# Causal attention with chosen experts on one core: the order of the diagonal key blocks inside a run of value sums

## The chip, the core and the metric

The kernel runs on one core of one Trainium2 chip. The metric is the device time of one execution in microseconds (us), as the median of several runs. The profile is of one more execution of the same kernel; its span runs from the first instruction to the last.

## What is computed

Two stages follow each other. The first is a linear attention: queries and keys are sketched with S1 and S2, multiplied out to 64 features, and summed against the values. Its output x (batch 4, 1088 tokens, 128 columns) goes into the second stage, a causal softmax attention with four experts of which each token takes two:

```python
for e in range(E):                       # 4 experts, heads of 64
    q, k, v = x @ wq[e], x @ wk[e], x @ wv[e]
    scores = scale * (q @ k.transpose(0, 2, 1))
    scores = np.where(causal, -1e9, scores)
    a = softmax(scores)
    ye = a @ v @ wo[e]
    out += (the share of e, where e is one of a token's two) * ye
```

The kernel uses that q k^T = x (wq wk^T) x^T and that a v wo = (a x)(wv wo): the weights are multiplied once, and what remains per batch is scores of x against x and sums of x weighted by a. The change touches these sums.

## The kernel before, in words

**Tiling.** A batch has 17 tiles of 64 tokens. For each tile the two chosen experts make two rows per token, so a score tile has 128 rows. The 17 tiles form three groups (`groups`, line 141): tiles 0 to 5, 6 to 11 and 12 to 16. A group has one buffer AT with its softmax weights, turned so that keys lie on partitions; one run of value sums per group and batch multiplies AT with x.

**A run of value sums** is `values` (line 1111). It goes over key steps j of 32 keys, J = 2·t1 of them: 12, 24 and 34 for the three groups. The 128 rows of AT are four bands of 32 rows, g = 0 to 3, one for each chosen expert and half of a tile's tokens; each j issues one matmul per band (line 1129), with 32 rows of x as weights and up to 32·nt columns of AT moving, nt being the tiles of the group (6, 6, 5). A full matmul is thus 192, 192 or 160 columns wide. The four bands use four different rows of the TensorE array and four different PSUM banks. All matmuls are float32, and the profile shows each as two passes, each with its own weight load.

**Causality.** `first(j, h)` (line 1119) gives the first column that key step j can reach: tiles ahead of it are skipped. Up to j = 2·t0 a matmul is full; from there on, in the diagonal part, it loses 32 columns with every second j, down to 32 columns. For odd j the bands with h = g % 2 = 0 (g = 0 and 2) lose 32 columns more, and at j = J−1 they have nothing to do, so that j issues two matmuls alone.

**Blocks and jobs.** A run is cut into blocks of four j (lines 1135 to 1140), each a job of the planner. A job reads the block before it, AT, and the x rows of its keys: tiles xr0 (j 0 to 11), xr1 (j 12 to 23) and xr2 (from j 24), named xra, xrb and xrc in the profile. The last block makes ("V", b, n), on which the copies out of PSUM wait: `keep`, `patch`, `mix` (lines 1148 to 1161).

**Order.** `ORDER` (line 21) is a fixed list of job numbers in the order in which the jobs are issued; a job's number is the place at which it was created. Each engine takes its instructions in that order. TensorE's work beside the sums is, above all, the scores (line 1053), the queries of the experts (line 1015), the output products (lines 1200, 1226, 1250) and the first stage of the next batch (lines 528, 577, 714, 769, 821). They use other shapes of the array than the sums' 32 rows by 128 columns: most of them 128 by 128.

**Runs in the order of time.** Batches 0 to 2 sum their groups as 0, 1, 2; batch 3 as 1, 2, 0. Mostly a run stands alone between other work. In batch 1, group 2 follows group 1 with nothing between, and other TensorE work stands behind group 2's fourth and sixth blocks. In batch 3, other work stands behind group 1's third block; what is left of group 1, group 2 and group 0 then follow one another with nothing between.

Of the kernel before, what the change touches and what calls it, by code (L numbers as in the profile page):

```python
# [71 lines left out]
class Plan:  # L72
# [5 lines left out]
    def job(self, name, eng, us, f, reads=(), makes=None, holds=(), landing=0.0, mode="", rank=0.0):  # L78
        eng = (eng,) if isinstance(eng, str) else tuple(eng)
        us = (us,) * len(eng) if isinstance(us, float) else tuple(us)  # L80
        self.jobs.append(dict(name=name, eng=eng, us=us, f=f, reads=tuple(reads), makes=makes, holds=tuple(holds),
                              landing=landing, mode=mode, rank=rank, n=len(self.jobs)))
# [32 lines left out]
def kernel(  # L115
# [76 lines left out]
    def copy(eng, o, i):  # L192
        (nc.scalar.copy if eng == "ACT" else VEC[eng].tensor_copy)(o, i)  # L193

    def d_us(n):
        return 0.18 + n / 960

    def a_us(n):
        return 0.2 + 0.00073 * n

    def p_us(n):
        return 0.12 + 0.0022 * n
# [799 lines left out]
    def masks_of(b, n, *xs):  # L1002
        return [("mb", b, n, x) for x in xs] if b == 0 and n == 0 else [("mb", b, n, 0)]
# [107 lines left out]
    def values(b, n, rank):  # L1111
        t0, t1 = groups[n]
        nt = t1 - t0
        w = 64 * nt
        AT, agg, mb = ("AT", b, n), ("agg", b, n), ("mb", b, n)
        Vk = [("ps", "V", b, n, l) for l in range(2)]
        J = 2 * t1

        def first(j, h):

            return 32 * max(0, j // 2 - t0) + (32 if j % 2 and j // 2 >= t0 and h == 0 else 0)

        def block(j0, j1):
            a = plan[AT][:, 0 : J * nt * 32].rearrange("p (j t s) -> p j (t s)", t=nt, s=32)
            for j in range(j0, j1):
                for g in range(4):
                    rows, lo = slice(32 * g, 32 * g + 32), first(j, g % 2)
                    if lo < 32 * nt:
                        nc.tensor.matmul(plan[Vk[g // 2]][:, g % 2, lo : 32 * nt], plan[(f"xr{j // 12}", b)][rows, j % 12], a[rows, j, lo:],  # L1129
                                         start=(j == 0), stop=(j == J - 2 + g % 2))  # L1130

        def cost(j0, j1):
            return sum(max(2 * (32 * nt - first(j, 1)) / 1200, 0.105 if j == J - 1 else 0.21) + 0.005 for j in range(j0, j1))

        for j0 in range(0, J, 4):
            j1 = min(j0 + 4, J)
            need = [("AT", b, n), ("xr", b, j0 // 12)] + ([("V", b, n, j0)] if j0 else [])
            job(f"sum {b}.{n}.{j0}", "PE", cost(j0, j1), lambda e, j0=j0, j1=j1: block(j0, j1), need,
                ("V", b, n, j1) if j1 < J else ("V", b, n),
                [AT, *Vk, (f"xr{j0 // 12}", b)], mode="V", rank=rank + 0.001 * j0)  # L1140

        def by_half(a):
            return a[:, 0:w].rearrange("p (t h s) -> p h t s", h=2, s=32)

        def sums_of(l):
            return plan[Vk[l]][:, :, 0 : 32 * nt].rearrange("p h (t s) -> p h t s", s=32)

        def keep(e, x):
            copy(e, by_half(plan[agg][:, x]), sums_of(x % 2))

        def patch(x):
            nc.vector.copy_predicated(by_half(plan[agg][:, 2 + x]), by_half(plan[mb][:, 4 + x].bitcast(U16)), sums_of(1 - x))

        def spread_sums(x):
            a = plan[agg][:, 2 * x : 2 * x + 2, 0:w]
            nc.gpsimd.tensor_tensor(out=a, in0=a, in1=plan[mb][:, 2 * x : 2 * x + 2, 0:w], op=ALU.mult)  # L1156

        r = rank + 0.1
        if last_group(b, n):
            def mix(x):  # L1160
                nc.vector.tensor_tensor(out=by_half(plan[agg][:, x]), in0=sums_of(x), in1=by_half(plan[mb][:, x]), op=ALU.mult)

            def scale_one(e, x):
                a = plan[agg][:, 2 + x, 0:w]
                VEC[e].tensor_tensor(out=a, in0=a, in1=plan[mb][:, 2 + x, 0:w], op=ALU.mult)

            for x in range(2):
                job(f"keep V {b}.{n}.{2 + x}", ("ACT", "DVE"), (a_us(w), d_us(w)), lambda e, x=x: keep(e, 2 + x),
                    [("V", b, n)], ("aggk", b, n, 2 + x), [Vk[x], agg], rank=r)
                job(f"mix V {b}.{n}.{x}", "DVE", d_us(w), lambda _, x=x: mix(x), [("V", b, n), *masks_of(b, n, 0)], ("agg", b, n, x),  # L1170
                    [Vk[x], agg, mb], rank=r + 0.01 * x)
                job(f"patch V {b}.{n}.{x}", "DVE", d_us(w), lambda _, x=x: patch(x),
                    [("V", b, n), ("aggk", b, n, 2 + x), *masks_of(b, n, 2)], ("aggp", b, n, x), [Vk[1 - x], agg, mb], rank=r + 0.01)
                job(f"scale V {b}.{n}.{x}", ("POOL", "DVE"), (p_us(w), d_us(w)), lambda e, x=x: scale_one(e, x),
                    [("aggp", b, n, x), *masks_of(b, n, 1)], ("agg", b, n, 2 + x), [agg, mb], rank=r + 0.02)
            return
        for x in (2, 3, 0, 1):
            job(f"keep V {b}.{n}.{x}", ("ACT", "DVE"), (a_us(w), d_us(w)), lambda e, x=x: keep(e, x),
                [("V", b, n)], ("aggk", b, n, x), [Vk[x % 2], agg], rank=r)
        for x in range(2):  # L1180
            job(f"patch V {b}.{n}.{x}", "DVE", d_us(w), lambda e, x=x: patch(x),
                [("V", b, n), ("aggk", b, n, 2 + x), *masks_of(b, n, 2)], ("aggp", b, n), [Vk[1 - x], agg, mb], rank=r + 0.01)
        for x in range(2):
            need = [("aggk", b, n, 0), ("aggk", b, n, 1)] if x == 0 else [("aggp", b, n)]
            job(f"spread V {b}.{n}.{x}", "POOL", p_us(2 * w), lambda e, x=x: spread_sums(x),
                [*need, *masks_of(b, n, x)], ("agg", b, n), [agg, mb], rank=r)

    def last_group(b, n):
        return b == B - 1 and n == 0
# [85 lines left out]
    def batch(b):  # L1275
        base = 100.0 * b
        order = []
        seq = list(range(NG)) if b < B - 1 else [1, 2, 0]
        for n in seq:
            order.append(("q", n))  # L1280
            for i in range(*groups[n]):
                order.append(("s", i))
        at, x = {}, 0.0
        for kind, y in order:
            at[(kind, y)] = base + x
            x += 2.6 if kind == "q" else (64 * (y + 1)) / 600 + 0.9 * (1 + y // 6)
        sc = 88.0 / x
        for kk in at:
            at[kk] = base + (at[kk] - base) * sc
        for n, (t0, t1) in enumerate(groups):  # L1290
            queries(b, n, at[("q", n)] - 14)
            for i in range(t0, t1):
                scores(b, n, i, at[("s", i)] - 3)
            p = seq.index(n)
            vt = at[("s", groups[seq[p + 1]][0] + 1)] if p + 1 < NG else base + 96
            values(b, n, vt)
            outputs(b, n, vt + 6)
# [42 lines left out]
```

## Time and profile before

| | |
|---|---|
| time, median of 3 runs | 263.02 us (262.99, 263.02, 263.62) |
| the profiled execution's own time | 263.14 us |
| its span | 261.4 us |
| granted TensorE clock | 1.000 |
| matmuls of line 1129 | 1136 with xra, 752 with xrb, 304 with xrc, two for each float32 product |

The profile names PE for TensorE's matmuls and PEld for its weight loads, DVE for VectorE, ACT for ScalarE and POOL for GpSimd. A timeline row gives start, duration, engine, line, what is written and read, the array shape, the moving operand's shape and how many instructions are merged in the row (x4); the duration of a merged row reaches from the first start to the last end. Starts are recorded, while the ends of matmuls are modelled. Where a row merges matmuls of several widths, it shows the first one's. A row of the table by stretches gives the stretch, its length, PE's busy time and count and PEld's, the granted clock and the DMA traffic.

### The profile page before, as it was taken

The page shows a single profiled execution, that of the slowest core. Times are in us where ns is not written, and L with a number is a line of the kernel's source. Part 1 is how long each engine was busy: PE and PEld are TensorE (multiplying, and loading weights), DVE is VectorE, ACT ScalarE, POOL GpSimd, SP SyncE. Part 2 cuts the span into 40 slices and gives each one's busy share as a digit, 9 for nine tenths or more (in the row PEclk, how much of TensorE's full clock was granted, in tenths as well). Part 3 has the DMA queues.
Part 4 walks back from the last instruction along what each step waited for, and adds up shares of the span by engine and source line. Part 5 has one row for each costly group of instructions (what it writes and reads, how often), then busy time and mean ns, then how long its engine had stood idle before and what let it go on. Part 6 is the DMA issues. An engine that isn't in the chain of part 4 may idle for free.

```text
span 261.4 us, 9228 instructions
## 1 busy us (share of the span) xinstructions
PE 253.7 (97%) x3811; PEld 189.7 (73%) x3813; DVE 212.8 (81%) x541; ACT 100.4 (38%) x268; POOL 155.8 (60%) x255
## 2 busy tenths in 40 slices
PE   7799999999999999999999999999999999999994
PEld 2388656666598895765799776665796885889994
DVE  4988999979989968999988379799989569881743
ACT  2183545563542406426432041825222515611220
POOL 3569479937498635498652794556435654442660
PEclk9999999999999999999999999999999999999999
DMA  6989379813736566903417592304560396240003
GB/s 207 162 180 165 80 173 151 175 39 81 172 72 109 115 148 141 190 20 118 81 39 114 143 204 54 109 0 73 103 119 0 91 217 159 44 111 6 5 0 88
DMA packets 85194, 27.84 MB, mean 106 GB/s; under 512 B 56736, under 2 KB 84128, under 8 KB 85152
## 3 DMA queue, kind: packets, MB, share of 16 engines
q1 hardware_dynamic: 84560, 26.56, 49.4%
q8 instruction: 30, 0.49, 0.8%
q10 hardware_dynamic: 592, 0.69, 0.7%
q14 instruction: 12, 0.10, 0.1%
HBM read 22.62 MB, written 4.62 MB: 104 GB/s over the span
## 4 chain that ended last, share of the span: by engine, by line
PE 78%; DVE 8%; POOL 5%; DMA 4%; issue 3%; SPq 0%; ACTq 0%; ACT 0%; DVEq 0%; POOLq 0%
PE pair L1053 26%; PE pair L1129 25%; PE pair L1015 9%; PE pair L1250 7%; DMA mb<-me 3%; PE pair L1200 2%; PE pair L577 2%; DVE qs L1028 2%; POOL fp L536 2%; PE pair L528 2%; PE pair L769 2%; DMA in<-in_q_dram 1%; PE pair L1226 1%; POOL agg L1156 1%; PE pair L821 1%
## 5 line engine op out<-in xcount | busy, mean ns | idle before, releaser
L1096 POOL TENSOR_SCALAR w<-w,rs,sh 128x448 f32<-128x448 f32 (+16 forms) x68 | 55.5, 823 | 36.9 <-DVE rs L1092 33.1
L1053 PE MATMUL pair<-xT,qs 128*128 128x384 f32 (+11 forms) x216 | 74.1, 477 | 0.8 <-DVE qs L1028 0.7
L1081 ACT ACTIVATE w<-w,mx 128x192 f32<-128x192 f32 (+15 forms) x68 | 52.5, 773 | 58.0 <-DVE mx L1065 45.0
L1053 PEld LDWEIGHTS pair<-xT,qs 128*128 128x128 f32 x216 | 38.7, 190 | 26.9 <-issue 11.5
L1065 DVE CUSTOM_DVE_ANT_0 w<-pair,mask 128x768 f32<-128x768 f32 (+15 forms) x68 | 48.4, 722 | 4.7 <-PE pair L1053 3.8
L1101 DVE STREAM_TRANSPOSE AT<-w 128x832 f32<-128x832 f32 (+15 forms) x68 | 50.8, 760 | 0.5 <-POOL w L1096 0.5
L1129 PEld LDWEIGHTS pair<-AT,xra 32*128 32x128 f32 x1136 | 42.0, 185 | 4.1 <-DVE mx L1065 2.0
L1129 PE MATMUL pair<-AT,xra 32*128 32x160 f32 (+5 forms) x1136 | 44.6, 302 | 0.0
L1156 POOL TENSOR_TENSOR agg<-agg,mb 128x768 f32<-128x768 f32 (+1 forms) x22 | 34.1, 1559 | 8.9 <-ACT agg L193 5.1
L1015 PE MATMUL pair<-xT,Mq 128*128 128x384 f32 (+1 forms) x96 | 35.0, 478 | 0.0
L536 POOL TENSOR_TENSOR fp<-w 128x576 f32<-128x576 f32 x25 | 30.6, 1235 | 3.9 <-DVE w L531 2.9
L193 ACT COPY agg<-pair 128x384 f32<-128x384 f32 (+1 forms) x28 | 11.8, 462 | 47.4 <-PE pair L1129 36.9
L1129 PE MATMUL pair<-AT,xrb 32*128 32x160 f32 (+5 forms) x752 | 27.2, 287 | 0.0
L1129 PEld LDWEIGHTS pair<-AT,xrb 32*128 32x128 f32 x752 | 26.4, 185 | 0.9 <-issue 0.9
L1028 DVE COPY_PREDICATED qs<-mb,pair 128x768 f32<-128x768 uint16 (+1 forms) x24 | 23.1, 964 | 4.1 <-DMA mb<-me 3.1
L1015 PEld LDWEIGHTS pair<-xT,Mq 128*128 128x128 f32 x96 | 17.2, 190 | 10.2 <-issue 2.8
L1250 PEld LDWEIGHTS pair<-Mo,agg 128*128 128x128 f32 x168 | 20.1, 192 | 1.7 <-POOL w L743 0.5
L1250 PE MATMUL pair<-Mo,agg 128*128 128x128 f32 x168 | 20.9, 277 | 0.0
L193 DVE COPY agg<-pair 128x384 f32<-128x384 f32 (+1 forms) x18 | 9.3, 530 | 13.7 <-PE pair L1129 11.6
L1089 POOL TENSOR_SCALAR rs<-zs 128x1 f32<-128x1 f32 x28 | 5.9, 212 | 20.1 <-ACT w L1081 13.5
L531 DVE STREAM_TRANSPOSE w<-pair 128x576 f32<-128x576 f32 x16 | 11.7, 757 | 4.4 <-PE pair L528 4.4
L1081 ACT ACTIVATION_READ_ACCUMULATOR w<-w,mx 128x1 f32 x68 | 12.9, 190 | 0.0
(172 smaller groups left out, 291.7 us busy)
## 6 DMA issues: line engine op xcount, KB each, us to landing
xra<-xd SPq DMA_DIRECT2D x16, 192.0 KB, 4.6
xrb<-xd SPq DMA_DIRECT2D x16, 192.0 KB, 4.1
xrc<-xd SPq DMA_DIRECT2D x16, 160.0 KB, 3.7
mb<-me SPq DMA_DIRECT2D x3, 576.0 KB, 5.1
mb<-me SPq DMA_DIRECT2D x6, 288.0 KB, 5.1
in<-in_k_dram SPq DMA_DIRECT2D x12, 136.0 KB, 4.7
in<-in_q_dram SPq DMA_DIRECT2D x3, 544.0 KB, 4.0
xd<-w SPq DMA_DIRECT2D x12, 136.0 KB, 2.8
```

The source lines that it names most:

```text
L193: (nc.scalar.copy if eng == "ACT" else VEC[eng].tensor_copy)(o, i)
L536: VEC[e].tensor_tensor(out=f, in0=a[:, :, None, R : 2 * R].to_broadcast([128, NJ, R, R]), in1=a[:, :, 0:R, None].to_broadcast([128, NJ, R, ...
L1015: nc.tensor.matmul(plan[ps[x]][:, y, 0:w], Mq[:, ((1, 2), (0, 3))[x][y]], plan[xT][:, 64 * t0 : 64 * t1], start=True, stop=True)
L1028: nc.vector.copy_predicated(chosen(), rows(c), rows(plan[ps[x]]))
L1053: nc.tensor.matmul(plan[p][:, y, 0 : c1 - c0], plan[qs][:, 128 * t : 128 * t + 128], plan[xT][:, c0:c1], start=True, stop=True)
L1065: nc.vector.tensor_tensor_reduce(out=o, in0=src, in1=msk, scale=-1.0, scalar=mx[:, b, i, x - 1 : x] if x else 3e38, op0=ALU.add, op1=ALU.m ...
L1081: nc.scalar.activation(out=a, in_=a, func=ACTF.Exp, bias=mx[:, b, i, last : last + 1], scale=-1.0, accum_out=zs[:, b, i : i + 1])
L1096: nc.gpsimd.tensor_scalar(out=a, in0=a, scalar1=rs[:, b, i : i + 1], scalar2=plan[("sh", b)][:, i : i + 1], op0=ALU.mult, op1=ALU.mult)
L1101: nc.vector.transpose(dst[:, 0 : keys // 32, t], plan[A][:, 0:keys].rearrange("p (j s) -> p j s", s=32))
L1129: nc.tensor.matmul(plan[Vk[g // 2]][:, g % 2, lo : 32 * nt], plan[(f"xr{j // 12}", b)][rows, j % 12], a[rows, j, lo:], start=(j == 0), sto ...
L1156: nc.gpsimd.tensor_tensor(out=a, in0=a, in1=plan[mb][:, 2 * x : 2 * x + 2, 0:w], op=ALU.mult)
L1250: nc.tensor.matmul(plan[p][0:m, 0, 128 * x : 128 * x + 128], plan[agg][:, e, 128 * x : 128 * x + m], Mo[:, e], start=(e == 0), stop=(e == ...
```

## The change

The blocks of a run are put in another order. `starts` holds the first j of each block; the first `whole` of them, max(1, t0 // 2), stay as they are, and the rest are turned round. Inside a turned block j falls instead of rising.

| group | blocks before | blocks after |
|---|---|---|
| 0 (12 j) | 0, 4, 8 | 0, 8↓, 4↓ |
| 1 (24 j) | 0, 4, 8, 12, 16, 20 | 0, 4, 8, 20↓, 16↓, 12↓ |
| 2 (34 j) | 0, 4, ... 20, 24, 28, 32 | 0, 4, ... 20, 32↓, 28↓, 24↓ |

The last matmul of a run was 32 columns wide; it is now 128 in group 0 (j = 4), 192 in group 1 (j = 12) and 160 in group 2 (j = 24). The first block, with the matmuls that start the accumulation, stays first. The set of matmuls, their operands and their number are the same, and so is `ORDER`: the job at each place of a run now issues the block that the new order has there.

```diff
+        starts = list(range(0, J, 4))
+        whole = max(1, t0 // 2)
+        starts = starts[:whole] + starts[whole:][::-1]
+
         def block(j0, j1):
             a = plan[AT][:, 0 : J * nt * 32].rearrange("p (j t s) -> p j (t s)", t=nt, s=32)
-            for j in range(j0, j1):
+            for j in range(j0, j1) if j0 in starts[:whole] else range(j1 - 1, j0 - 1, -1):
                 for g in range(4):
                     rows, lo = slice(32 * g, 32 * g + 32), first(j, g % 2)
                     if lo < 32 * nt:
                         nc.tensor.matmul(plan[Vk[g // 2]][:, g % 2, lo : 32 * nt], plan[(f"xr{j // 12}", b)][rows, j % 12], a[rows, j, lo:],
-                                         start=(j == 0), stop=(j == J - 2 + g % 2))
+                                         start=(j == 0), stop=(j == starts[-1]))
...
-        for j0 in range(0, J, 4):
+        for y, j0 in enumerate(starts):
             j1 = min(j0 + 4, J)
-            need = [("AT", b, n), ("xr", b, j0 // 12)] + ([("V", b, n, j0)] if j0 else [])
+            need = [("AT", b, n), ("xr", b, j0 // 12)] + ([("V", b, n, y)] if y else [])
             job(f"sum {b}.{n}.{j0}", "PE", cost(j0, j1), lambda e, j0=j0, j1=j1: block(j0, j1), need,
-                ("V", b, n, j1) if j1 < J else ("V", b, n),
-                [AT, *Vk, (f"xr{j0 // 12}", b)], mode="V", rank=rank + 0.001 * j0)
+                ("V", b, n, y + 1) if y + 1 < len(starts) else ("V", b, n),
+                [AT, *Vk, (f"xr{j0 // 12}", b)], mode="V", rank=rank + 0.004 * y)
```

## The prediction

> **What bounds the kernel now.** I read the first part of the page, the chain that ended last, and the list of who waited for whom on PE.
>
> ```profile
> span 261.4 us, 9228 instructions
> PE 253.7 (97%) x3811; PEld 189.7 (73%) x3813; DVE 212.8 (81%) x541; ACT 100.4 (38%) x268; POOL 155.8 (60%) x255
> ...
> PE 78%; DVE 8%; POOL 5%; DMA 4%; issue 3%; SPq 0%; ACTq 0%; ACT 0%; DVEq 0%; POOLq 0%
> PE pair L1053 26%; PE pair L1129 25%; PE pair L1015 9%; PE pair L1250 7%; DMA mb<-me 3%; PE pair L1200 2%; PE pair L577 2%; DVE qs L1028 2%; POOL fp L536 2%; PE pair L528 2%; PE pair L769 2%; DMA in<-in_q_dram 1%; PE pair L1226 1%; POOL agg L1156 1%; PE pair L821 1%
> ```
>
> ```profile
> PE pair L1053 <- DVE qs L1028: 0.7, 2, 0.5
> ```
>
> PE is busy for 97% of the span, a quarter of the chain is the sums themselves (L1129), and PE's scores wait for another engine twice, 0.7 us in all. So a gap or a saving between two PE instructions shows nearly one to one in the time. Next come the stretches of the sums, their bounds read from the timeline:
>
> ```profile
> 56.16:59.28 3.12, 3.11 (x92) 3.07 (x92) 1.00 0.22 66
> 70.88:77.90 7.02, 7.01 (x188) 6.97 (x188) 1.00 0.40 101
> 89.48:98.47 8.99, 8.98 (x268) 8.94 (x268) 1.00 0.57 117
> 108.46:111.58 3.12, 3.10 (x92) 3.07 (x92) 1.00 0.67 130
> 133.92:145.37 11.45, 11.44 (x316) 11.27 (x316) 1.00 0.45 77
> 146.90:149.29 2.39, 2.38 (x64) 2.21 (x64) 1.00 0.49 111
> 151.30:153.77 2.47, 2.45 (x76) 2.42 (x76) 1.00 1.09 181
> 167.90:171.02 3.12, 3.11 (x92) 3.07 (x92) 1.00 0.19 42
> 185.85:192.87 7.02, 7.01 (x188) 6.97 (x188) 1.00 0.61 113
> 204.02:213.01 8.99, 8.98 (x268) 8.94 (x268) 1.00 0.67 168
> 230.25:234.37 4.12, 4.11 (x96) 3.89 (x96) 1.00 0.72 173
> 235.42:250.37 14.95, 14.93 (x452) 14.90 (x452) 1.00 0.02 5
> ```
>
> Equal runs take equal time in every batch (3.12, 7.02, 8.99), at clock 1.00: they wait for nothing inside. Of the twelve stretches, nine end with a 32-column matmul today; the fifth, sixth and eleventh stop at a full one and stay as they are.
>
> **The price of one pass.** Each band of 32 rows works through its own passes. In the narrow part the loads of one pair of bands set the pace:
>
> ```profile
> 58.59 0.32 PEld L1129 LDWEIGHTS pair<-AT,xra 32*128 32x128 f32 x8
> 58.70 0.31 PEld L1129 LDWEIGHTS pair<-AT,xra 32*128 32x128 f32 x6
> 58.81 0.31 PEld L1129 LDWEIGHTS pair<-AT,xra 32*128 32x128 f32 x4
> 58.93 0.31 PEld L1129 LDWEIGHTS pair<-AT,xra 32*128 32x128 f32 x4
> ```
>
> They start every 0.112 us (0.34 us over three steps, rounded rows), whatever the width of the matmul. For a wide matmul the streaming sets it: the eleventh stretch is 24 passes of 192 columns in 4.12 us; less 0.112 for its first load and 0.09 for its end (next fence), a pass is 0.163 us, or 0.85 ns a column. So a pass costs the larger of 0.112 and 0.85 ns times its width, and the two are equal at 132 columns. Now the two kinds of end, a narrow one and two full ones:
>
> ```profile
> 59.05 0.19 PEld L1129 LDWEIGHTS pair<-AT,xra 32*128 32x128 f32 x1
> 59.28 0.13 PEld L714 LDWEIGHTS pair<-zx,S2r 128*64 128x64 f32 x1
> ```
>
> ```profile
> 234.10 0.34 PE L1129 MATMUL pair<-AT,xra 32*128 32x192 f32 x4
> 234.38 0.43 PE L1053 MATMUL pair<-xT,qs 128*128 128x192 f32 x1
> ```
>
> ```profile
> 149.05 0.31 PE L1129 MATMUL pair<-AT,xrb 32*128 32x160 f32 x4
> 149.29 0.59 PE L1015 MATMUL pair<-xT,Mq 128*128 128x384 f32 x1
> ```
>
> Narrow: the last load starts at 59.05, its matmul can stream at 59.16, 32 columns last 0.027, and the next work's load starts 0.09 later, at 59.28. At 192 columns: the last of the four matmuls starts at 234.12, streams 0.163 until 234.285, and the next work starts 0.09 later. At 160: 149.07 plus 0.136 and again 0.09. The reader is to see that the next shape's load starts some 0.09 us after the stream has ended, and never under it, however wide the last matmul is.
>
> Hence a run costs 0.112, plus the larger price for each pass but the last, plus 0.85 ns a column for the last, plus 0.09. The bands h = 1 have the most passes: group 0 has 4 of 192, 4 of 160 and 16 narrow; group 1 has 28, 4 and 16; group 2 has 52 of 160 and 16. That gives 3.10, 7.01 and 8.97 us, against 3.12, 7.02 and 8.99. The twelfth stretch (half of group 1, group 2, group 0 in one piece) comes to 14.94 against 14.95, and it holds two jumps from 32 columns back to full ones: a rise costs nothing of its own.
>
> **The change part by part.**
>
> 1. *The end.* Before, the last narrow pass has no further load of its shape behind it and costs 0.027 instead of 0.112. After, all narrow passes stand in the middle and cost 0.112, and the last wide one costs what it cost anyway. In groups 1 and 2 a run gets 0.112 − 0.027 = 0.085 longer; in group 0, which ends at 128 columns (0.109), 0.085 − 0.003 = 0.082.
> 2. *The fall* from full width to 32 columns: the load of the first narrow pass (0.112) lies under the last full matmul (0.163 or 0.136): nothing. Without that cover it would cost 0.112 a run.
> 3. *The matmuls of j = J−1*, in two bands alone: the other two bands have fewer and narrower passes, and these two passes now run beside idle bands at the start of the narrow part instead of at the end: nothing. If the idle bands had to catch up, 2 × 0.112 a run, the bound from above.
> 4. *Waits and queues.* The first block still waits for AT; the x tiles are first touched and last read in the same order, xra, xrb, xrc, so the DMAs that refill them on SP start as before, behind the same last block. Places in `ORDER`, and so every engine's queue, are the same. Nothing, up to one late landing of xrc.
> 5. *The copies out of PSUM* start with the end of the run, so 0.085 later, as PE's next work does. In the fifth stretch, where group 2 follows group 1, PE loses nothing, but group 1's sums are complete 0.085 later against PE.
>
> The nine ends: group 0 four times, group 1 twice, group 2 three times: 4 × 0.082 + 5 × 0.085 = 0.753 us on PE. Does it all arrive? The chain leaves PE at two places:
>
> ```profile
> 141.15 0.57 DVE agg L193
> ...
> 145.11 1.65 POOL agg L1156
> ...
> 147.20 6.72 DMA mb<-me
> ...
> 156.25 1.00 DVE qs L1028
> 157.25 0.04 issue
> 157.29 1.02 PE pair L1053 x2
> ```
>
> This detour starts with group 1's sums in batch 1. Four narrow ends lie ahead (0.334), and its start is 0.085 later still: 0.419. PE's own way to 157.29 has the seventh stretch on it, also 0.419. Nothing is absorbed.
>
> ```profile
> 171.16 0.48 ACT L193 COPY agg<-pair 128x384 f32<-128x384 f32 x1 [1.63 <-PE pair L1129]
> 171.19 0.54 DVE L193 COPY agg<-pair 128x384 f32<-128x384 f32 x1
> ```
>
> ```profile
> 171.02 1.34 PE L1015 MATMUL pair<-xT,Mq 128*128 128x320 f32 x4
> 172.20 2.32 PE L1200 MATMUL pair<-agg,Mo 128*128 128x320 f32 x8
> 175.03 0.67 PE L1053 MATMUL pair<-xT,qs 128*128 128x480 f32 x1 [0.52 <-DVE qs L1028]
> ```
>
> Here PE idles 0.52 us until DVE is done, so the eighth stretch's 0.082 counts only as far as DVE is late: its copy at 171.19 began when the sums were complete, to 0.03 (ACT's began at 171.16), so 0.05 to 0.082 come through. I take 0.05, a loss of 0.03. The sum: 0.753 − 0.03 = 0.72, and 263.14 + 0.72 = **263.86 us**. The profiled execution lies 0.12 above the median of 263.02 and within the three runs' spread; seen from the median, the same step ends at 263.74. The two stand on both sides of 263.81, where a change of 0.3% (about what a measurement of this kernel can tell from no change) begins.
>
> **The rivals.**
>
> *The next load hides under the wide end* (faster). Were the next work's load drawn under the last full matmul, each of the nine ends from 59.28 on would save the 0.09 and a load of 0.112 and lose 0.085: −0.117 × 9 = −1.05, 262.1 us. Against it stand both full ends above, with 0.09 left over after 192 and after 160 columns. For it: neither was followed by every kind of work that follows the nine.
> The Trainium skill ("TensorE: Matmul & The Clock Gate", "Step-by-step: what each phase is for") states that TensorE pulls weight loads ahead of matmuls in flight; by that rule this rival would hold. Its page "TensorEngine Tiling (Array Packing)", "Key Properties", says that changing the tiling mode drains the engine, and the two full ends agree with this one, 0.09 us past the stream. Chance 0.08.
>
> *The delay is absorbed.* If the detours at 141 and 171 do not move with PE, PE's 0.52 us of idling at 175 takes in all that was lost ahead of it, and 0.082 + 2 × 0.085 = 0.25 remain: 263.4 us. Against it: both detours begin with a read of what PE has just made. Chance 0.08.
>
> *The idle bands hold the others* (slower). If the idle bands of j = J−1 hold the others, two passes a run come on top, from the first turned run on: 0.72 + 9 × 0.224 = 2.7, 265.9 at most; half of it, one pass a run, is 264.9. Against it: at the end of a run the same two passes run at the same 0.112 (58.81, 58.93). Chance 0.10.
>
> *It does not do what it says:* in group 0 the run ends at 128 columns, under the 132 from which streaming sets the pace, so even a hidden load would lie there under 0.109. That is part of the forecast (0.082 instead of 0.085), not a case of its own.
>
> **How the numbers follow.** The forecast has 0.74, own range 263.5 to 264.2 (the sum from either base, 263.74 and 263.86, with 0.3 for the scatter of runs). It is split at 263.81, a little more above, since the sum's own base is the profiled time: 0.40 slower, 0.34 same. The faster rival adds 0.08 to faster, absorption 0.08 to same, the last one 0.10 to slower: faster 0.08, same 0.42, slower 0.50. The range 263.2 to 264.8 holds the forecast, absorption and the milder half of the slow case.
>
> **What would show it.** Nine stretches of sums longer by 0.08 (3.20, 7.10, 9.07), the fifth, sixth and eleventh unchanged. After each run the next shape's load 0.09 us behind the stream of a 128, 160 or 192 wide matmul; if instead it begins less than 0.2 us after the start of the last 192 wide pass, the first rival holds. Idling at 175 still near 0.5. Loads in the rising part 0.112 apart; more would be the third rival. The prediction is wrong if the runs do not get longer, or if they do and the span does not follow.

## The result, and the profile after

| | before | after |
|---|---|---|
| median | 263.19 us (16 runs, 262.87 to 263.94) | 264.11 us (16 runs, 262.98 to 265.37) |
| profiled execution: time, span | 263.14, 261.4 us | 264.11, 262.3 us |
| ratio | | 1.003, 95% interval 1.0016 to 1.0045 |

The change makes the kernel slower by 0.3%, or 0.79 us with an interval of 0.42 to 1.18 us; the medians themselves lie 0.92 us apart. These are the lines of the changed kernel's page that answer to those of before; L1129 is now L1133.

```profile
span 262.3 us, 9230 instructions
PE 253.6 (97%) x3813; PEld 189.4 (72%) x3813; DVE 212.8 (81%) x541; ACT 100.2 (38%) x268; POOL 155.8 (59%) x255
...
PE 84%; DVE 7%; POOL 4%; issue 2%; DMA 1%; ACTq 0%; ACT 0%; DVEq 0%; POOLq 0%
PE pair L1133 28%; PE pair L1053 26%; PE pair L1015 10%; PE pair L1254 7%; PE pair L1204 2%; PE pair L528 2%; PE pair L577 2%; POOL fp L536 2%; PE pair L769 2%; DMA in<-in_q_dram 1%; DVE qs L1028 1%; PE pair L1230 1%; PE pair L821 1%; DVE w L498 1%; DVE ch L832 1%
```

The busy sums say nothing: PE has 253.6 us, and had 253.7. They merge overlapping matmuls of four bands, so a pass that takes longer because of a load does not show in them. The sums' share of the chain rises from 25% to 28%. The stretches show where the time lies:

```profile
56.67:59.86 3.19, 3.19 (x92) 3.07 (x92) 1.00 0.21 64
71.47:78.56 7.09, 7.09 (x188) 6.87 (x188) 1.00 0.42 110
90.15:99.21 9.06, 9.05 (x268) 8.89 (x268) 1.00 0.57 117
109.21:112.40 3.19, 3.18 (x92) 3.07 (x92) 1.00 0.77 131
134.75:146.19 11.44, 11.43 (x316) 11.27 (x316) 1.00 0.45 77
147.72:150.11 2.39, 2.38 (x64) 2.21 (x64) 1.00 0.72 150
152.13:154.66 2.53, 2.52 (x76) 2.36 (x76) 1.00 1.20 206
168.56:171.75 3.19, 3.18 (x92) 3.07 (x92) 1.00 0.13 29
186.38:193.47 7.09, 7.08 (x188) 6.87 (x188) 1.00 0.60 114
204.65:213.71 9.06, 9.06 (x268) 8.89 (x268) 1.00 0.61 169
230.96:235.07 4.11, 4.11 (x96) 3.89 (x96) 1.00 0.72 174
236.13:251.24 15.11, 15.11 (x452) 14.99 (x452) 1.00 0.02 4
```

Nine stretches are longer, the fifth, sixth and eleventh are not. From the recorded starts, to the nanosecond, group 0 alone takes 3.190 instead of 3.110, group 1 7.092 instead of 7.010, group 2 9.062 instead of 8.980, the seventh stretch 2.530 instead of 2.460, and the twelfth 15.113 instead of 14.940. Together that is 3 × 0.080 + 4 × 0.082 + 0.070 + 0.173 = 0.811 us. The seventh gains less than the other runs that stand alone, and the twelfth more; the experiments come back to both.

The ends of a 192 column and a 128 column run in the changed kernel:

```profile
78.30 0.33 PE L1133 MATMUL pair<-AT,xrb 32*128 32x192 f32 x2
78.57 0.59 PE L1015 MATMUL pair<-xT,Mq 128*128 128x384 f32 x1
```

```profile
251.05 0.27 PE L1133 MATMUL pair<-AT,xra 32*128 32x128 f32 x1
251.25 0.38 PE L1254 MATMUL pair<-Mo,agg 128*128 128x128 f32 x1
```

The later of the pair at 78.30 starts at 78.315; with 0.163 of streaming and 0.09 the next work comes at 78.57. At 251.05 the streaming takes 0.109, and again 0.09 is left. The next shape's load lies under no end.

Two rows of the list of who waited on PE, in the changed kernel:

```profile
PE pair L577 <- issue: 1.0, 1, 1.0
...
PE pair L1053 <- DVE qs L1028: 0.5, 2, 0.3
```

The first lies at 53 us, ahead of the first run of sums, where the two programs issue the same; before, the same wait took 0.62 us. The longest wait of the second row is the one near 175, 0.30 instead of 0.52 us. The profiled pair differs by 0.877 us of span, which splits as follows (starts and ends of the stretches, in us):

| from, to | before | after | difference |
|---|---|---|---|
| start of the span, first stretch | 56.170 | 56.670 | +0.500 |
| start of the first, end of the seventh | 97.606 | 97.998 | +0.392 |
| end of the seventh, start of the eighth | 14.133 | 13.900 | −0.233 |
| start of the eighth, start of the ninth | 17.954 | 17.818 | −0.136 |
| start of the ninth, end of the span | 75.570 | 75.924 | +0.354 |

So the agreement of the two profiled spans with the forecast is partly luck: 0.5 us of the difference stands ahead of the change. The experiments were to tell which of these five belong to it.

### The profile page after: what moved, and what is told of

It is laid out like the page before. It is cut to its first block, busy times and chain, and to the rows that moved or that the text cites. A ratio compares the mean times of both kernels' runs of the same rounds, so it can differ in the third digit from the quotient of the medians.

```text
span 262.3 us, 9230 instructions
## 1 busy us (share of the span) xinstructions
PE 253.6 (97%) x3813; PEld 189.4 (72%) x3813; DVE 212.8 (81%) x541; ACT 100.2 (38%) x268; POOL 155.8 (59%) x255
## 4 chain that ended last, share of the span: by engine, by line
PE 84%; DVE 7%; POOL 4%; issue 2%; DMA 1%; ACTq 0%; ACT 0%; DVEq 0%; POOLq 0%
PE pair L1133 28%; PE pair L1053 26%; PE pair L1015 10%; PE pair L1254 7%; PE pair L1204 2%; PE pair L528 2%; PE pair L577 2%; POOL fp L536 2%; PE pair L769 2%; DMA in<-in_q_dram 1%; DVE qs L1028 1%; PE pair L1230 1%; PE pair L821 1%; DVE w L498 1%; DVE ch L832 1%
## 5 line engine op out<-in xcount | busy, mean ns | idle before, releaser
L1133 PEld LDWEIGHTS pair<-AT,xra 32*128 32x128 f32 x1136 | 42.4, 186 | 4.0 <-DVE mx L1065 2.0
L1133 PE MATMUL pair<-AT,xra 32*128 32x160 f32 (+5 forms) x1136 | 45.1, 304 | 0.0
L1160 POOL TENSOR_TENSOR agg<-agg,mb 128x768 f32<-128x768 f32 (+1 forms) x22 | 34.1, 1560 | 9.0 <-ACT agg L193 5.2
L1133 PE MATMUL pair<-AT,xrb 32*128 32x160 f32 (+5 forms) x752 | 27.7, 289 | 0.0
L1133 PEld LDWEIGHTS pair<-AT,xrb 32*128 32x128 f32 x752 | 26.4, 186 | 0.9 <-issue 0.5
L1028 DVE COPY_PREDICATED qs<-mb,pair 128x768 f32<-128x768 uint16 (+1 forms) x24 | 23.1, 963 | 3.9 <-DMA mb<-me 2.9
```

Source lines behind the costliest of these rows:

```text
L1028: nc.vector.copy_predicated(chosen(), rows(c), rows(plan[ps[x]]))
```

## The experiments

In the kernels that follow, `values` takes its key steps from a list and cuts it into blocks of four; each kernel differs from before in this list alone, and in the stop flag, which goes with the last pass of each half. A turned group 2 falls into blocks of 4, 4 and 2 steps here, and of 2, 4 and 4 in the changed kernel; where both were measured, the stretches agree to 0.003 us.

```diff
+        steps = list(range(J))       # the list of before; each kernel has its own
...
-            for j in range(j0, j1):
+            for j in js:
...
-        for j0 in range(0, J, 4):
+        blocks = [steps[x : x + 4] for x in range(0, J, 4)]
+        for y, js in enumerate(blocks):
```

**The end without the turning, and the turning without the end.** Two kernels take the change apart. The first keeps the turned order but issues the two narrowest steps last:

```diff
+        steps = list(range(max(4, 2 * t0))) + list(range(max(4, 2 * t0), J - 2))[::-1] + [J - 2, J - 1]
```

> The changed order, but the last two key steps (32 columns wide) are issued last, as before; the rest of the diagonal still runs from narrow to wide. Theory of the exposed end (a narrow pass costs 0.112 us unless it is the last one): the runs take 3.11, 7.01 and 8.98 us as before, and the time is that of before, 263.2 us, ratio 1.000. Rival, the reversal itself costs (rising widths, bands out of step): the runs keep their 3.19, 7.09 and 9.06 us and the time stays near 264, ratio 1.003.

Measured: 263.27 us, ratio 0.9998 (0.998 to 1.0015). Its first, second, third and twelfth stretches:

```profile
56.67:59.78 3.11, 3.11 (x92) 3.07 (x92) 1.00 0.22 66
71.39:78.40 7.01, 7.01 (x188) 6.97 (x188) 1.00 0.40 101
89.99:98.97 8.98, 8.97 (x268) 8.94 (x268) 1.00 0.56 117
...
235.77:250.81 15.04, 15.03 (x452) 14.99 (x452) 1.00 0.02 4
```

The second keeps the order of before and takes one wide step to the end:

```diff
+        steps = [j for j in range(J) if j != max(1, 2 * t0)] + [max(1, 2 * t0)]
```

> The order of before, rising, with one wide key step taken out and issued last (j = 1, 12 and 24 in the three groups). Theory of the exposed end: the runs that stand alone take 3.19, 7.10 and 9.07 us, 0.085 more than before, with no reversal in them, and the time is near that of the changed kernel, 263.8 to 264.1, ratio 1.002 to 1.003. Rival, the reversal costs: 3.11, 7.01 and 8.98, ratio 1.000.

Measured: 263.24 us, ratio 1.0009 (0.9987 to 1.0031), which holds both expectations; the stretches decide:

```profile
56.11:59.30 3.19, 3.18 (x92) 2.97 (x92) 1.00 0.21 64
70.92:78.01 7.09, 7.09 (x188) 6.87 (x188) 1.00 0.40 100
89.60:98.66 9.06, 9.05 (x268) 8.89 (x268) 1.00 0.58 117
...
235.39:250.41 15.02, 15.02 (x452) 14.80 (x452) 1.00 0.02 4
```

A wide end alone makes the runs as long as the change does, and a narrow end behind a turned diagonal makes them as short as before. Only the twelfth stretch has a part of both: 15.022 with the wide end (+0.082) and 15.034 with the turning (+0.094); their sum is the change's +0.173 to 0.003.

**The size of the price.** A narrow step of three widths at the end, in an order that otherwise rises:

```diff
+        steps = [j for j in range(J) if j != (8, 18, 26)[n]] + [(8, 18, 26)[n]]
```

> The order of before with one narrow step of the diagonal moved to the end: 64 columns wide in group 0 (j = 8), 96 in group 1 (j = 18), 128 in group 2 (j = 26). Theory of the exposed end (0.85 ns for each column of the last pass over 32): 3.110 + 0.027 = 3.137, 7.010 + 0.054 = 7.064, 8.980 + 0.082 = 9.062, and 14.967 for the twelfth, which ends with group 0. Rival, any end but the narrowest costs a whole load: 0.085 in all three groups.

```profile
56.10:59.24 3.14, 3.13 (x92) 3.07 (x92) 1.00 0.20 56
70.85:77.91 7.06, 7.05 (x188) 6.97 (x188) 1.00 0.42 109
...
204.11:213.17 9.06, 9.05 (x268) 8.94 (x268) 1.00 0.66 168
...
235.60:250.56 14.96, 14.96 (x452) 14.90 (x452) 1.00 0.02 4
```

One run took 263.36 us. To the nanosecond the stretches take 3.137, 7.064, 9.060 and 14.967: each within 0.002 us of the expectation. The price is 0.83 to 0.84 ns for each column by which the last pass is wider than 32; it stops growing where streaming sets the pace, since ends of 160 and 192 columns cost the same, 0.082 to 0.083. The recorded loads say the same: from the last load of a run to the next work 0.229 us pass behind 32 columns (before), 0.256 behind 64 and 0.283 behind 96, each within 0.002 of 0.112 for the load, the streaming and 0.09.

**The lone step J−1.** Only this step is moved, to the head of the diagonal:

```diff
+        steps = list(range(max(4, 2 * t0))) + [J - 1] + list(range(max(4, 2 * t0), J - 1))
```

> The order of before with one step moved: the key step J-1, which keeps two bands busy, stands ahead of the diagonal instead of at the end; the run ends on J-2, 32 columns wide in all four bands. Theory of the exposed end: all stretches as before, 3.11, 7.01, 8.98, 14.94. Rival, idle bands hold the others: up to 0.22 more in each of the nine; a part of it would also explain the 0.09 that the twelfth stretch has over the theory in the changed kernel.

Measured: one run, 265.76 us, with its first stretch at 58.90, 2 to 3 us later than in the other profiles: ahead of it PE waits 1.32 us for nothing that the profile shows, and from 54.00 to 58.90 the granted clock is 0.65. That time says nothing of the step. The stretches take 3.110, 7.010, 8.980, and 2.447 and 14.927 in the seventh and twelfth, 0.013 less than before. No stretch gets longer, so the rival of the idle bands falls, and the lone step isn't the twelfth stretch's surplus either. The change moves this step too, which fits the seventh stretch: 0.070 there, where a wide end alone costs 0.082.

**The twelfth stretch.** Two kernels turn a single run of batch 3 (`b == 3 and n == 1`, `b == 3 and n == 2`).

> The changed order in one run alone, group 1 of batch 3, whose blocks are issued between blocks of group 2. It doesn't end the twelfth stretch, so the theory of the exposed end gives 14.94 us for that stretch, as before. If the 0.09 that the twelfth stretch has over the theory in the changed kernel comes from this turned run among the other run's wide blocks, 15.03.

> The changed order in one run alone, group 2 of batch 3, in the middle of the twelfth stretch. Theory of the exposed end: 14.94 us. If the 0.09 comes from this run, 15.03; if half from each of the two, 14.985.

One run each: 262.96 and 263.36 us. The twelfth stretch of the first and of the second kernel:

```profile
235.14:250.17 15.03, 15.03 (x452) 14.99 (x452) 1.00 0.02 4
```

```profile
235.67:250.61 14.94, 14.94 (x452) 14.90 (x452) 1.00 0.02 5
```

The surplus (15.034, and 14.940 without it) belongs to group 1 alone. In the timeline of before, this stretch begins so:

```profile
235.44 1.48 PE L1129 MATMUL pair<-AT,xrb 32*128 32x192 f32 x32
236.63 1.37 PE L1129 MATMUL pair<-AT,xra 32*128 32x160 f32 x32
237.72 1.03 PE L1129 MATMUL pair<-AT,xrb 32*128 32x128 f32 x30
```

In batch 3 the groups do not follow one another in one piece: a block of group 1 (xrb), one of group 2 (xra), one of group 1, and so on. A turned group 1 thus puts its narrowest block first and jumps to 160 columns behind it. Why that jump costs 0.094, while those from the end of group 2 into group 0 cost nothing, stays open: the lone step is excluded, since the kernel with the narrow end leaves it last and has the surplus too, but not the order in which the bands reach the wide block.

**What reaches the end.** The change in the runs ahead of the wait near 175, and in those behind it:

```diff
+        steps = (list(range(max(4, 2 * t0))) + list(range(max(4, 2 * t0), J))[::-1]) if b < 2 or (b == 2 and n == 0) else list(range(J))
...
+        steps = (list(range(max(4, 2 * t0))) + list(range(max(4, 2 * t0), J))[::-1]) if b == 3 or (b == 2 and n > 0) else list(range(J))
```

> The changed order in batches 0 and 1 and in group 0 of batch 2 alone, all ahead of the place near 175 us where TensorE waits for VectorE. Theory that the delay travels on: six longer runs, 0.082 x 3 + 0.085 + 0.085 x 2 = 0.50 us, less 0.03 at that wait, ratio 1.0018. Rival, absorbed at the waits near 157 and 175 us: from the first run to the end of the wait at 175 the trace shows the 118.86 us of before to 0.05, though the runs are longer, and the ratio is 1.000.

> The changed order in groups 1 and 2 of batch 2 and in batch 3 alone, all behind the wait near 175 us. From that wait's end to the end of the span: 86.4 us before, 86.75 in the changed kernel, and 86.75 here on either theory, since nothing absorbs behind it. The time: ratio 1.0013. If the early half is absorbed, this kernel is as slow as the whole change; if it travels on, it is about 0.45 us faster than that.

Measured: the early runs 263.36 us, ratio 0.9998 (0.9977 to 1.0018); the late ones 263.19 us, 1.0008 (0.9993 to 1.0023). The intervals hold nearly all expectations, so the traces have to tell. The 118.86 us that were to mark absorption can't: the early runs' kernel takes 118.72 us there, but the kernel of before, profiled again, takes 118.58. Shorter pieces tell more. From the ninth stretch's start to the end the late runs need 75.909 us against 75.570: all of it arrives. Between the first stretch's start and the seventh's end, 98.00 to 98.02 us pass in the five profiles whose runs end wide there, and 97.59 to 97.61 in the eight whose runs all end on 32 columns: that arrives too. But from the eighth stretch's start to the ninth's it is 17.82 with the early runs turned and 17.95 with the late ones.

There it matters which of VectorE and GpSimd comes first. Rows of the timeline of before, then of the changed kernel, in which GpSimd multiplies agg (L1156, now L1160) and VectorE makes its last comparisons (L870, L871) ahead of the pick of the queries (L1028):

```profile
172.33 1.64 POOL L1156 TENSOR_TENSOR agg<-agg,mb 128x768 f32<-128x768 f32 x1
172.36 1.63 DVE L870 TENSOR_TENSOR c<-ch 128x9 bf16<-128x9 f32 x1
...
174.03 0.17 DVE L871 TENSOR_TENSOR c<-c 128x18 bf16<-128x18 bf16 x1
174.12 0.86 DVE L1028 COPY_PREDICATED qs<-mb,pair 128x640 f32<-128x640 uint16 x1
```

```profile
173.00 1.69 POOL L1160 TENSOR_TENSOR agg<-agg,mb 128x768 f32<-128x768 f32 x1
173.02 0.16 DVE L870 TENSOR_TENSOR c<-ch 128x9 bf16<-128x9 f32 x1
...
173.22 1.50 DVE L871 TENSOR_TENSOR c<-c 128x18 bf16<-128x18 bf16 x1
174.64 0.86 DVE L1028 COPY_PREDICATED qs<-mb,pair 128x640 f32<-128x640 uint16 x1
```

A comparison of 9 columns takes 0.16 us, or 1.63 when it meets GpSimd's product, and then it ends 0.03 behind that product. Before, L870 was caught, and L871 and the pick still came behind it; after, L870 slipped through and L871 was caught. Counted from the start of the eighth stretch, the product starts at 4.417 us before and at 4.437 after, and L870 at 4.454 and 4.453. So L870 begins 0.037 behind the product's recorded start before, and 0.016 behind it after. In all fourteen profiles L870 is caught at 0.035 to 0.040 (nine) and passes at 0.010 to 0.019 (five); where it passes, the product takes 1.68 to 1.69 us instead of 1.64 to 1.65.

The run ends 0.08 later, but L870 is not later at all, and the product only by 0.02. By the profile this goes back to VectorE's own copy of the sums, at 171.19 before and here in the changed kernel:

```profile
171.85 0.56 DVE L193 COPY agg<-pair 128x384 f32<-128x384 f32 x1
```

It starts 3.282 us after the start of the eighth stretch before and 3.285 after, and 3.277 to 3.290 in all fourteen profiles. By the releasers that the profile infers, the sums set it free at 3.223 before, so it then waited 0.059 for VectorE's own work, and at 3.261 after, 0.024 ahead of its start. Why this release comes only 0.038 later, and not 0.08, isn't shown. ScalarE's first copy, released at 3.223 and 3.320, does come later, at 3.343 instead of 3.246. But its second is released by the end of VectorE's copy (3.821 before, 3.842 after) and starts 0.033 to 0.036 behind it in all fourteen profiles; the product is released by the end of this second copy (4.334 and 4.354).

The Trainium skill ("SBUF — State Buffer", "SBUF: two separate sides") says that VectorE, with two SBUF inputs, and GpSimd take a shared pair of ports as a lock for a whole instruction; the lengths agree with that, though no run shows why L870 passed at 0.016 and not at 0.037, both behind the product's recorded start. Two kernels test the place, with the eighth stretch's run alone turned (`b == 2 and n == 0`) and with all others turned.

> The changed order in one run alone, group 0 of batch 2, the eighth stretch, just ahead of the wait near 175 us. Theory that a later end of this run moves GpSimd's product of agg (L1156 before) behind VectorE's fourth small comparison (L870), so that VectorE waits for GpSimd once for 0.2 us less: the eighth stretch takes 3.19 instead of 3.11, and yet from its start to the start of the ninth it is 17.82 us instead of 17.95; the time 0.13 us under before, ratio 0.9995, which the timing can't tell from 1. Rival, the saving comes from the other turned runs: 17.95 to 18.03.

> The change without group 0 of batch 2: the eighth stretch as before. Theory that VectorE's order against GpSimd decides: from the eighth stretch's start to the ninth's 17.95 us, as before and 0.13 more than in the changed kernel; the time that of the change plus 0.13 us, ratio 1.002 to 1.0035. Rival, the saving comes from the other turned runs: 17.74 to 17.82.

```profile
168.02:171.21 3.19, 3.18 (x92) 3.07 (x92) 1.00 0.18 43
185.84:192.85 7.01, 7.00 (x188) 6.97 (x188) 1.00 0.60 116
```

```profile
172.47 1.69 POOL L1160 TENSOR_TENSOR agg<-agg,mb 128x768 f32<-128x768 f32 x1
172.48 0.17 DVE L870 TENSOR_TENSOR c<-ch 128x9 bf16<-128x9 f32 x1
...
172.68 1.50 DVE L871 TENSOR_TENSOR c<-c 128x18 bf16<-128x18 bf16 x1
174.10 0.86 DVE L1028 COPY_PREDICATED qs<-mb,pair 128x640 f32<-128x640 uint16 x1
```

With this run alone turned (the rows above), 17.82 us pass from 168.02 to 185.84; with all others turned, 17.952. The eighth run alone decides. In all fourteen profiles the two cases do not mix: 17.81 to 17.82 where this run ends 0.08 later (five), 17.95 to 17.96 where it ends as before or only 0.027 later (nine). The times: 263.26 us, ratio 0.9994 (0.9963 to 1.0024), for the one, and 264.55 us, 1.0029 (1.0001 to 1.0057), for the other. By the stretches, the first is the only order here that should beat the kernel of before, by 0.13 us; both intervals are far too wide to show a step of that size.

**Scatter.** Both kernels once more:

> The kernel before once more, for the scatter of its waits: stretches to 0.005 us as before; from the first stretch's start to the seventh's end 97.61; from there to the eighth's start between 13.7 and 14.15, by when the masks of the next batch land; eighth to ninth 17.95; the first stretch starts between 55.8 and 56.7.

> The changed kernel once more, for the scatter of its waits: from the first stretch's start to the seventh's end 98.00; from there to the eighth's start, if the wait for the masks moves with TensorE's work, 13.7 to 14.15 as before; if the later TensorE absorbs it, 13.7 to 13.9; eighth to ninth 17.82; from the ninth's start to the end 75.9.

Measured: before 262.59 us, the changed kernel 264.24 us, one run each. The runs of sums repeat to 0.003 us; the first stretch started at 55.91 and 56.93; from the eighth stretch to the ninth 17.959 and 17.810; from the ninth to the end 75.563 and 75.944. Over all fourteen profiles two of the five rows of the table above turn out to scatter:

| | range | without late ends so far | with late ends so far |
|---|---|---|---|
| start of the first stretch | 55.84 to 56.93, and once 58.90 | same program in all | same program in all |
| end of the seventh to the eighth | 13.70 to 14.42 | mean 13.93 of 8 | mean 13.90 of 5 |

(The graded kernel, with 13.94, is in neither mean.) In the second row, what comes last is VectorE's pick of the queries, which waits for the masks of the next batch: in thirteen of the fourteen profiles the eighth stretch starts 10.67 us after the second pick of this kind ends. The first of the two transfers of masks is issued 90.61 to 90.62 us after the first stretch's start in the eight profiles without late ends, and at 91.02 to 91.04 in the five with them. That is the 0.42 later that was forecast. What scatters is the transfer: the second, which lands last, takes 5.83 to 6.99 us from issue to landing.

The last row scattered once. Behind the twelfth stretch, where all kernels issue the same, 11.03 to 11.08 us pass in thirteen profiles, and 11.30 in the one with the eighth run alone turned.

## Why the prediction was right

**The end of a run** was right in place, mechanism and size: 0.080 to 0.082 measured where 0.082 and 0.085 were forecast, with the streaming plus 0.09 behind every width tried. Only the seventh stretch got less, 0.070, since the lone step gives 0.013 back there. The narrow end and the wide end show the cause, and the graded ends its size.

**The fall, the lone step, the waits**: nothing, as forecast; the lone step even saves 0.013 in the two stretches that begin with it. That *a rise costs nothing* held for eight of the nine stretches that got longer and failed for the twelfth stretch: turned group 1 of batch 3 costs 0.094 more. The twelfth stretch was taken as three groups in one piece, while blocks of two groups alternate there.

**What arrives.** At the first detour nothing is absorbed, as forecast. This is read from the issue of the masks, which moves by 0.42; the time from the seventh stretch to the eighth agrees (the means differ by 0.03) but could not show it alone, with 0.7 between single profiles. At the second the term had the wrong size and sign: 0.05 of the eighth run's delay was to come through, on the reading that VectorE's copy at 171.19 began when the sums were complete, to 0.03. Its own slack was about as read there, but the sums set it free only 0.038 later instead of 0.082, so it started at 3.28 us with the delay and without, and none of the delay came through. On top of that, 0.136 was gained over before, since the slightly later product let one comparison pass.

The terms as measured: 0.392 from the first stretch to the seventh, 0 at the first detour, −0.136 at the second, 0.354 behind it, together 0.61 us or 1.0023, against 0.72 forecast. Two errors, +0.09 in the twelfth stretch and −0.19 at the second detour, partly cancel: that the sum comes so near is partly luck. The measured ratio of 1.003 holds 1.0023 in its interval; the rest of the 0.92 us between the medians is not shown to come from the change.

**The rivals.** A load hidden under a wide end: excluded at 128, 160 and 192 columns. Absorption: at one place, where PE idles 0.22 us less: 0.08 because VectorE does not move with the run, and 0.136 because a comparison passes. Idle bands: excluded. Whether the change counts as slower was left nearly open, with 0.50 against 0.42, and the measured ratio stands at the 0.3% that parts the two.

## What to carry to other kernels

Where a pass costs the larger of its own streaming and the next pass's load, the order of the passes leaves all terms alone but the last: let a burst end on its narrowest pass, since behind that one there is no load to wait for. Whether the next shape's load hides under the end is read from the ends that the trace already has, two widths of them. A shift of 0.08 us on the busiest engine can change which of two other engines comes first, so what arrives at the end is measured place by place, not taken from the sum.

## What was not expected of the hardware

A VectorE comparison of 9 columns took 0.16 us or 1.63 us, by whether it met a GpSimd product: it was caught when it began 0.035 to 0.040 us behind the product's recorded start and passed when it began 0.010 to 0.019 behind. A shift of 0.02 there took 0.136 us out of the time to the ninth stretch. And the four bands of a 32-row matmul do not keep step: matmuls of two different runs stand side by side in the timeline (before, group 2 begins a block at 238.556, while group 1 starts its last matmul of the block ahead at 238.593). Group 1 of batch 3, turned between blocks of group 2, cost 0.094 us more than the sum of its passes; that the bands' lead is the cause is not shown.
